# A new instruction order, new buffer slots and other fillers for a fused polysketch-attention and wave-MLP kernel

## The chip, the cores and the metric

The kernel runs on one core of one Trainium2 chip. The metric is the device time of one execution in microseconds; the profile is of one execution of the same program, recorded by the hardware profiler. The core's engines work side by side, each through its own list of instructions in order: PE (TensorE: matmuls, and PEld, the loading of their weights), DVE (VectorE), ACT (ScalarE), POOL (GpSimd) and SP (SyncE, which only issues DMAs here). An engine that needs another's result waits for a semaphore. The results of matmuls go to PSUM, eight banks; everything else lies in SBUF.

## The reference

Four batches, four heads, 1088 positions, head dimension 32 (so a row of 128), sketch size 8. Attention by polynomial sketches comes first, then an MLP that mixes positions.

```python
def phi(x):
    a = np.einsum('rd,bhsd->bhsr', S1, x)
    b = np.einsum('rd,bhsd->bhsr', S2, x)
    return np.einsum('bhsi,bhsj->bhsij', a, b).reshape(*x.shape[:-1], r * r)
q_p, k_p = (phi(q), phi(k))
kv = np.einsum('bhsf,bhsd->bhfd', k_p, v)
z = np.sum(k_p, axis=2)
num = np.einsum('bhsf,bhfd->bhsd', q_p, kv)
den = np.einsum('bhsf,bhf->bhs', q_p, z)[..., None] + 1e-06
x = (num / den), heads joined to rows of 128

theta = x @ w_theta
zr = x * np.cos(theta)
zi = x * np.sin(theta)
y = np.einsum('ts,bsd->btd', w_tok_r, zr) + np.einsum('ts,bsd->btd', w_tok_i, zi)
u = x + y
out = u + np.maximum(u @ w_ch, 0.0)
```

The weights `w_tok_r`, `w_tok_i` (1088 x 1088), `w_theta`, `w_ch`, `S1` and `S2` come as float64. [...]

## The kernel before

The kernel is written as a list of 1022 operations, made by calls of `op(engine, cost, function, writes, reads)`. An operation is one or some instructions on one engine: P is TensorE, V VectorE, A ScalarE, G GpSimd, S SyncE. They are numbered from 0 in the order in which the program text makes them. Nothing is run in that order. `Layout.run` takes three strings from the top of the file: `ORDER` lists all 1022 numbers in the order in which they are issued, so that an engine's own list is what remains of it when the other engines' numbers are struck out; `PLACES` gives each of the 419 temporary buffers its slot within its class (22 slots of class `big`, 5 of `zs`, 6 of `hf`, 8 PSUM banks `ps`, and so on); `SPINS` names operations ahead of which so many filler matmuls are put (`spin`, L379: 384 columns of zeros, bf16, into a PSUM bank that is not read). Semaphores are set where one engine's operation needs another's result, or a slot that another's operation still reads.

The stages, for each batch b:

- Loads (SyncE): k, q and v, 576 KB each (`load`, L614), 17 rows of w_tok, 1088 KB each, and w_sq (both small weight matrices, 256 KB); the last two in `weight` (L583). ScalarE turns each row to float32 in two passes (L584 with the function Prelu, L586 with Copy, about 1.2 us each), and VectorE joins them in two (L588 and L590).
- Scales: operations 4 to 28 bring in S1 and S2 and scale them. Operation 9 is ScalarE's second conversion of them (L424), 10 VectorE's product after it, 16 the scaling itself (L469). Operation 3 is a sine of one number that nobody reads (`warm`, L384).
- Keys (`key_sums`, `kfeatures`), the chains that find the sketches' exact slices (`chain`; 174 is the second product in that of batch 1), and query slices (`query_slices`).
- `levels`: three groups of matmuls per batch (420 to 424 for batch 0, 517 to 521 for batch 1, 648 to 652 for batch 2, 719 to 723 for batch 3), three copies to SBUF by ScalarE (L1002), then ten operations of VectorE that make numerator and denominator, stage "den" (725 to 734 for batch 3).
- `outputs_x`: per group of three chunks of 128 positions an outer product on VectorE, its transpose, the numerator matmul and its copy (L1078; 677 for group 1 of batch 2). Batches 0 and 1 are transposed on TensorE; batches 2 and 3 by DMA (`turned`: VectorE's 32 x 32 transposes at L326, such as 736 for batch 3's group 0; a scatter to DRAM by DMAs that SyncE and ScalarE issue, L333, such as 737 and 738; and one DMA back, L338). Then theta: the matmul with w_theta (685, 696 and 707 for batch 2), for batch 2 the transpose of x by DMA too (686 on VectorE, 687 and 688 the scatter, 689 the way back), the rounding, Abs and two sines on ScalarE (L1114, L1115, L1117; 461 to 463 for group 0 of batch 0, 692 to 694 for group 0 of batch 2) and the product z = x (cos, sin) on VectorE (464, 695).
- Mixing: batches 0 and 1 run 17 rows of w_tok against z (`mix_row`; 482 to 498 are rows 0 to 16 of batch 0, three matmuls of up to 384 columns each). Batches 2 and 3 share seven products by Winograd's scheme (`winograd`, stages m1 to m7; 787 and 815 are the first matmuls of m1 and m2).
- Outputs: `finish` and `finish_turned` add x, multiply by w_ch, apply max and store; 1018 is the last matmul.

Ten fillers stand at the start (operation 1, L382). The order matters in every stage, since each engine waits at the head of its own list.

Of the kernel before, what the change touches and what calls it, by code (L numbers as in the profile page):

```python
# [26 lines left out]
TINY = 2.0**-60  # L27
UP = 256.0
ORDER = (
    "6 4 2 5 44 0 1 45 50 3 47 7 340 8 48 46 11 9 10 49 12 29 58 13 30 70 83 84 64 76 71 14 77 85 96 15 88 72 89 78 "  # L30
    "65 86 90 97 79 16 91 66 159 17 92 26 87 98 67 148 27 93 80 32 18 68 19 73 99 309 25 94 141 20 310 74 95 31 142 "
    "35 149 341 21 101 129 151 160 102 150 40 103 104 161 130 105 342 41 131 106 135 107 43 343 162 197 345 136 108 "
    "360 210 22 137 152 355 305 42 53 344 307 198 315 138 306 313 28 110 109 211 139 132 111 23 314 100 308 212 203 "
    "112 133 316 113 36 69 24 204 114 33 199 213 34 143 115 117 75 116 311 144 59 81 200 118 119 312 317 82 346 120 "
    "191 39 121 37 122 124 123 145 424 60 335 125 38 348 422 375 153 420 423 425 154 214 421 155 347 426 61 427 318 "
    "349 246 156 428 57 126 157 239 319 192 158 356 429 227 127 240 164 128 62 247 165 241 430 167 63 337 166 431 "
    "168 249 134 51 432 242 193 169 228 433 140 336 229 170 434 146 194 233 171 350 230 435 173 56 172 147 436 234 "
    "174 361 443 439 437 175 450 438 176 446 440 444 177 441 447 250 445 453 178 442 248 179 448 180 320 454 357 "
    "457 181 188 451 182 338 459 385 458 452 205 183 251 449 235 184 352 460 252 185 187 186 358 521 461 163 339 "
    "462 517 463 253 359 519 518 217 522 455 520 464 236 465 206 523 456 482 524 467 222 215 525 216 351 468 483 "  # L40
    "526 469 353 365 471 527 223 362 473 354 466 189 470 254 528 255 472 529 484 256 190 530 475 387 224 476 257 "
    "376 531 485 267 532 377 268 533 366 390 540 534 370 536 269 537 543 547 541 535 321 542 363 548 270 550 378 "
    "549 538 544 364 386 218 219 368 539 551 388 545 54 220 477 380 201 221 546 552 367 195 325 554 263 553 379 400 "
    "225 486 556 479 264 326 265 389 322 474 266 487 478 557 371 369 558 323 207 196 324 271 372 373 202 480 208 "
    "395 272 562 374 209 381 563 571 382 570 383 488 327 564 405 384 392 489 275 481 391 231 401 410 393 555 490 "
    "560 403 559 273 394 572 396 491 276 274 328 278 573 402 329 492 398 277 565 574 415 404 397 279 406 493 399 "
    "576 280 561 52 407 281 494 282 408 411 409 566 625 575 626 243 567 579 412 413 495 237 283 414 416 496 285 284 "
    "417 418 497 286 299 287 568 419 288 498 55 289 290 293 291 294 292 577 578 648 569 511 505 512 650 649 226 652 "
    "651 627 653 628 654 629 655 602 295 656 580 657 581 658 603 296 604 659 660 582 258 661 583 499 662 300 232 "
    "500 663 238 330 259 506 630 605 298 664 584 260 585 665 261 586 331 262 671 501 666 667 606 513 332 631 333 "  # L50
    "587 678 334 607 502 588 503 589 301 297 514 608 679 609 672 590 632 842 674 668 591 841 673 592 840 681 633 "
    "719 680 721 720 723 722 244 724 669 245 725 610 675 726 670 504 611 727 612 728 593 729 685 686 594 730 688 "
    "595 731 682 302 732 613 687 676 733 634 734 677 614 697 735 635 699 698 615 736 696 596 689 690 839 616 597 "
    "737 691 683 838 692 303 684 636 304 738 742 637 638 708 701 617 743 709 694 693 639 702 707 695 703 700 618 "
    "710 744 749 815 805 704 750 787 705 788 712 816 745 796 640 711 797 798 751 598 706 817 713 739 641 756 714 "
    "799 715 818 789 752 599 790 515 800 844 516 716 819 619 791 718 801 717 620 820 802 746 806 803 807 753 792 "
    "740 808 741 809 760 821 762 810 763 747 845 754 804 748 843 642 811 764 769 755 643 757 822 771 778 765 621 "
    "772 780 758 812 813 622 759 793 781 766 761 768 823 767 773 644 774 794 835 782 770 645 775 846 795 777 847 "
    "776 784 848 783 855 864 856 836 857 814 858 867 779 849 785 859 875 837 868 860 861 866 893 850 876 894 851 "
    "869 884 870 862 885 871 852 872 853 877 865 886 898 887 854 878 895 879 863 888 874 901 880 896 507 873 889 "  # L60
    "938 911 935 890 881 939 882 786 891 824 912 883 902 892 913 940 825 897 903 826 955 646 914 900 915 830 600 "
    "904 942 601 916 831 956 937 957 899 933 975 647 905 934 946 945 931 943 906 907 508 917 509 947 941 510 918 "
    "936 908 827 948 974 958 976 828 959 832 960 932 834 949 944 833 950 829 961 962 951 963 952 987 953 988 954 "
    "919 909 920 989 623 977 990 624 991 926 964 927 978 910 965 992 979 966 921 968 980 922 981 982 928 983 923 "
    "984 925 924 985 930 993 967 986 994 995 969 996 1007 971 929 1012 1013 1014 997 998 1015 999 1008 1000 1001 "
    "1009 1002 1003 1011 1010 1004 1005 970 1006 1016 1017 972 1018 1019 973 1020 1021 "
)
PLACES = (
    "7 0 1 5 0 10 17 16 14 0 15 5 6 15 18 0 10 3 5 0 11 5 3 4 3 6 3 6 2 2 8 4 4 0 5 12 0 6 12 4 12 4 6 5 4 7 1 5 8 "
    "5 10 8 4 4 1 5 9 0 8 8 5 2 0 4 1 6 10 1 0 1 1 4 2 4 0 3 1 4 6 0 4 3 5 1 3 2 21 2 10 6 5 8 3 5 4 3 5 12 4 1 0 2 "  # L70
    "3 2 9 2 0 6 4 4 1 2 1 0 4 2 3 7 3 5 3 3 5 2 4 4 4 6 4 5 4 1 3 5 0 2 3 5 2 0 8 12 1 7 0 7 0 11 4 2 12 7 2 5 5 8 "
    "3 5 3 1 5 4 2 8 12 3 0 3 2 4 3 5 0 1 0 2 4 4 1 7 4 5 3 0 3 19 0 11 13 2 11 8 2 5 16 0 10 2 1 4 7 4 1 11 0 10 3 "
    "4 1 5 3 15 17 1 20 14 1 17 20 3 0 1 4 15 6 0 18 0 1 10 18 3 10 9 0 10 0 6 1 5 6 0 12 2 0 0 0 6 6 2 2 1 4 4 1 0 "
    "7 0 1 6 5 4 1 4 1 4 5 0 0 3 6 5 0 2 4 4 1 3 7 2 0 3 5 4 21 1 21 4 3 4 2 5 7 2 3 7 4 7 1 2 5 2 2 4 7 2 7 1 3 2 "
    "5 4 1 1 0 2 5 3 4 5 4 0 5 5 0 5 2 3 4 6 12 1 3 1 1 2 4 0 2 3 2 3 3 6 5 0 4 1 2 3 0 0 0 6 3 0 0 3 0 7 10 1 10 3 "
    "1 2 2 0 3 1 1 6 3 0 4 5 0 0 3 5 4 6 4 2 6 5 2 5 3 2 0 5 4 15 7 1 6 5 7 0 5 0 1 5 1 6 7 2 6 0 1 7 3 3 1 4 2 5 2 "
)
SPINS = (
    "70:2 15:3 137:1 211:1 424:2 128:1 168:1 174:2 176:1 521:2 "
)  # L80
WARM = 0
SPLIT = ()
# [1330 lines left out]
```

## Time and profile before

| What | Value |
|---|---|
| Median of 3 runs | 219.76 us (219.3, 219.76, 219.84) |
| Span of the profiled execution | 217.4 us |
| Mean granted TensorE clock | 0.997 |
| DMA traffic | 40.58 MB, mean 187 GB/s |
| Longest waits: ScalarE's L1201 for TensorE | 42.5 us in 3 waits |
| Longest wait of a VectorE instruction in 5 to 100 us | 0.4 us, of L437 for TensorE's L436 |
| TensorE's waits that are put down to one instruction | 4.5 us in the ten largest kinds |

The span runs from the first instruction to the last; the runs' time includes what lies around it. A page gives each engine's busy time; the waits are put down to the semaphore that came last. ScalarE's 42.5 us lie at the end, where it has next to nothing to do. Idle time of an engine that nobody waits for costs nothing.

### The profile page before, as it was taken

The page shows a single profiled execution, that of the slowest core. Times are in us where ns is not written, and L with a number is a line of the kernel's source. Part 1 is how long each engine was busy: PE and PEld are TensorE (multiplying, and loading weights), DVE is VectorE, ACT ScalarE, POOL GpSimd, SP SyncE. Part 2 cuts the span into 40 slices and gives each one's busy share as a digit, 9 for nine tenths or more (in the row PEclk, how much of TensorE's full clock was granted, in tenths as well). Part 3 has the DMA queues.
Part 4 walks back from the last instruction along what each step waited for, and adds up shares of the span by engine and source line. Part 5 has one row for each costly group of instructions (what it writes and reads, how often), then busy time and mean ns, then how long its engine had stood idle before and what let it go on. Part 6 is the DMA issues. An engine that isn't in the chain of part 4 may idle for free.

```text
span 217.4 us, 5063 instructions
## 1 busy us (share of the span) xinstructions
PE 209.3 (96%) x1998; PEld 154.3 (71%) x1998; DVE 181.2 (83%) x408; ACT 111.2 (51%) x214; POOL 22.2 (10%) x44
## 2 busy tenths in 40 slices
PE   7999899999999999999999999999999999999994
PEld 3987786686766686666766575667758788888883
DVE  4899999999999999999599839988138999996542
ACT  3998498899779999983322040354037400000010
POOL 2237000055000000100132000100101000000000
PEclk9999999999999999999999999999999999999998
DMA  5999996869979979894226998599911000045253
GB/s 153 429 406 340 425 399 203 333 224 271 267 276 361 361 264 380 219 198 126 33 36 102 222 137 199 105 156 151 231 78 32 0 0 0 3 66 89 36 79 75
DMA packets 52635, 40.58 MB, mean 187 GB/s; under 512 B 45444, under 2 KB 47108, under 8 KB 50436
## 3 DMA queue, kind: packets, MB, share of 16 engines
q1 hardware_dynamic: 35540, 33.71, 48.7%
q0 software_dynamic: 1728, 4.65, 10.5%
q10 hardware_dynamic: 15344, 1.90, 6.0%
q8 instruction: 15, 0.25, 0.5%
q14 instruction: 8, 0.07, 0.1%
HBM read 30.43 MB, written 5.18 MB: 164 GB/s over the span
## 4 chain that ended last, share of the span: by engine, by line
PE 72%; DVE 12%; ACT 8%; DMA 4%; ACTq 2%; issue 2%; SPq 1%
PE ps L341 66%; DMA big<-q_l 2%; DVE lv L305 2%; PE ps L1064 2%; ACTq L333 2%; PE ps L1098 1%; DMA fx<-g 1%; DVE g L305 1%; DVE big L305 1%; PE ps L967 1%; ACT big L584 1%; ACT big L937 1%; DVE hf L309 1%; DVE zs L305 1%; ACT g L1068 1%
## 5 line engine op out<-in xcount | busy, mean ns | idle before, releaser
L341 PE MATMUL ps<-big,zs 128*128 128x384 f32 (+4 forms) x398 | 109.7, 424 | 0.4 <-DVE zs L305 0.4
L341 PEld LDWEIGHTS ps<-big,zs 128*128 128x128 f32 x398 | 71.4, 190 | 30.3 <-issue 2.6
L1201 ACT COPY g<-ps 128x128 f32<-128x128 f32 (+1 forms) x3 | 0.9, 301 | 42.5 <-PE ps L1193 42.5
L305 DVE CUSTOM_DVE_ANT_0 big<-big,big 128x2176 uint16<-128x2176 uint16 x17 | 21.8, 1287 | 0.4 <-ACT big L586 0.2
L584 ACT ACTIVATE big<-zs 128x1088 f32<-128x1088 f32 x17 | 20.9, 1235 | 2.1 <-DMA zs<-w_tok 1.2
L586 ACT ACTIVATE big<-zs 128x1088 int32<-128x1088 uint32 (+1 forms) x18 | 21.3, 1184 | 0.1
L341 PE MATMUL ps<-big,big 128*64 128x64 f32 (+2 forms) x208 | 20.6, 276 | 0.0
L341 PEld LDWEIGHTS ps<-big,big 128*64 128x64 f32 (+1 forms) x208 | 16.5, 154 | 2.9 <-issue 0.2
L305 DVE TENSOR_TENSOR big<-big,big 128x544 f32<-128x544 f32 x24 | 16.7, 712 | 0.0
L1002 ACT COPY lv<-ps 128x480 f32<-128x480 f32 x12 | 6.3, 563 | 14.2 <-PE ps L341 14.2
L312 DVE SCALAR_TENSOR_TENSOR g<-g,ps 128x384 f32<-128x384 f32 x12 | 6.6, 548 | 8.1 <-ACT g L1111 8.1
L1078 ACT COPY big<-ps 128x384 f32<-128x384 f32 x12 | 5.9, 489 | 14.0 <-PE ps L341 8.3
L309 DVE TENSOR_SCALAR big<-big 128x1088 int32<-128x1088 int32 x17 | 12.2, 724 | 0.6 <-ACT big L584 0.5
L341 PEld LDWEIGHTS ps<-w,big 128*128 128x128 f32 x80 | 10.6, 192 | 2.3 <-ACT g L1068 0.6
L319 POOL DMA_DIRECT2D big<-hf x6 | 5.4, 957 | 63.3 <-DVE g L312 33.8
L319 POOL DMA_DIRECT2D g<-big x6 | 5.2, 920 | 64.8 <-ACT g L1179 34.7
L341 PE MATMUL ps<-w,big 128*128 128x128 f32 x80 | 11.8, 280 | 0.0
L305 DVE TENSOR_TENSOR g<-lv 128x768 f32<-128x768 f32 x12 | 11.2, 945 | 0.0
L341 PE MATMUL ps<-g,sm 128*64 128x384 f32 x48 | 10.1, 507 | 0.2 <-ACT big L1078 0.2
L305 DVE TENSOR_TENSOR zs<-ps,g 128x768 f32<-128x768 f32 (+2 forms) x15 | 9.4, 632 | 1.0 <-PE ps L1098 0.9
L341 PEld LDWEIGHTS <-hf 128*64 128x64 f16 (+1 forms) x288 | 7.7, 110 | 2.9 <-issue 1.7
L379 PE MATMUL ps<-idle 128*128 128x384 bf16 x27 | 7.8, 400 | 1.3 <-POOL idle L381 1.3
(194 smaller groups left out, 336.6 us busy)
## 6 DMA issues: line engine op xcount, KB each, us to landing
zs<-w_tok SPq DMA_DIRECT2D x17, 1088.0 KB, 7.0
big<-k_l SPq DMA_DIRECT2D x6, 576.0 KB, 6.6
big<-hf POOLq DMA_DIRECT2D x6, 576.0 KB, 6.0
big<-v_l SPq DMA_DIRECT2D x4, 576.0 KB, 7.0
g<-fq SPq DMA_DIRECT2D x6, 384.0 KB, 5.2
big<-q_l SPq DMA_DIRECT2D x3, 576.0 KB, 5.1
fq<-g SPq DMA_DIRECT2D x12, 96.0 KB, 4.0
fq<-g ACTq DMA_DIRECT2D x12, 96.0 KB, 4.1
```

Of the source, the lines that this page charges most:

```text
L305: eng.tensor_tensor(out=o, in0=a, in1=b, op=f)
L309: (eng or V).tensor_scalar(out=o, in0=a, scalar1=s1, scalar2=s2, op0=op0, **kw)
L312: (eng or V).scalar_tensor_tensor(out=o, in0=a, scalar=s, in1=b, op0=op0, op1=op1)
L319: op("G", 0.9, lambda: G.dma_start(dst(), src(), accum_op=ALU.add), w, r, fly=fly)
L333: E.dma_start(there().rearrange("(a i) (x b j) -> b i x a j", a=nf, b=nf, j=SQ)[f], blocks()[f * SQ:(f + 1) * SQ].rearrange("i (x a j) -> ...
L341: T.matmul(o, lhs, rhs, start=start, stop=stop, skip_group_check=True)
L379: T.matmul(nowhere() if home is None else view(home, (GW,), F32), idle()[:, 0:P], idle(), start=True, stop=True, skip_group_check=True)
L584: op("A", 0.22 + n * 0.0009, lambda: A.activation(dfn(), words_of(raw(), n)[1].bitcast(F32), AF.Prelu, scale=2.0**-112, alpha=-(2.0**32)), ...
L586: op("A", 0.22 + n * 0.0009, lambda: A.activation(stp(), words_of(raw(), n)[0].bitcast(U32), AF.Copy, scale=2.0**-29), [stp], [raw])
L1002: op("A", act(480), lambda g=g, lp=lp: A.copy(lv().rearrange("p l (c n) -> p l c n", n=HR)[:, :, g * GC:(g + 1) * GC], lp().rearrange("p c ...
L1064: T.transpose(tr()[:, i * P:(i + 1) * P], qp()[:, i * H + 2 * n:i * H + 2 * n + 2].rearrange("p h i j -> p (h i j)"), ident())
L1078: op("A", act(GW), lambda g=g, xp=xp: A.copy(xt()[:, g * GW:(g + 1) * GW], xp()), cells(xt, g * GW, (g + 1) * GW), [xp])
```

## The change

Only the three strings differ. All 1022 operations, their functions and their dependences stay, and so does the rest of the file. `ORDER` is another sequence: of TensorE's 357 operations 34 keep their place in its list, of VectorE's 347 17, of ScalarE's 214 19. `PLACES` gives other slots. `SPINS` has 6 fillers ahead of four operations in place of 16 ahead of ten.

Core of the diff; lines of "..." are left out.

```diff
 ORDER = (
-    "6 4 2 5 44 0 1 45 50 3 47 7 340 8 48 46 11 9 10 49 12 29 58 13 30 70 83 84 64 76 71 14 77 85 96 15 88 72 89 78 "
...
-    "174 361 443 439 437 175 450 438 176 446 440 444 177 441 447 250 445 453 178 442 248 179 448 180 320 454 357 "
...
-    "462 517 463 253 359 519 518 217 522 455 520 464 236 465 206 523 456 482 524 467 222 215 525 216 351 468 483 "
...
-    "719 680 721 720 723 722 244 724 669 245 725 610 675 726 670 504 611 727 612 728 593 729 685 686 594 730 688 "
-    "595 731 682 302 732 613 687 676 733 634 734 677 614 697 735 635 699 698 615 736 696 596 689 690 839 616 597 "
-    "737 691 683 838 692 303 684 636 304 738 742 637 638 708 701 617 743 709 694 693 639 702 707 695 703 700 618 "
-    "710 744 749 815 805 704 750 787 705 788 712 816 745 796 640 711 797 798 751 598 706 817 713 739 641 756 714 "
...
+    "58 4 0 2 5 6 1 44 45 47 48 49 50 7 59 8 340 60 56 11 9 61 12 10 51 13 83 70 29 46 14 76 30 355 71 84 15 77 335 64 "
...
+    "326 128 375 230 315 431 236 211 432 199 171 433 200 242 321 173 172 434 316 174 322 212 435 175 450 176 177 453 178 "
...
+    "463 462 359 519 518 522 353 254 467 255 520 464 402 473 523 468 401 482 354 475 370 524 387 483 476 265 469 525 471 "
...
+    "723 680 681 669 721 670 724 686 614 675 722 688 687 641 725 615 726 642 581 245 727 643 582 728 685 682 729 583 690 "
+    "730 584 731 676 691 732 692 616 689 694 733 585 677 697 586 734 698 699 696 735 683 736 303 587 684 737 738 708 588 "
+    "749 589 709 693 304 590 710 695 591 750 700 787 644 742 752 707 842 592 712 815 713 816 743 788 593 844 711 745 796 "
...
+    "765 761 814 768 621 767 773 830 775 825 835 780 770 774 781 846 3 845 782 855 847 776 783 856 777 848 836 784 779 "
...
 )
 PLACES = (
-    "7 0 1 5 0 10 17 16 14 0 15 5 6 15 18 0 10 3 5 0 11 5 3 4 3 6 3 6 2 2 8 4 4 0 5 12 0 6 12 4 12 4 6 5 4 7 1 5 8 "
...
+    "3 6 2 0 5 11 6 2 12 5 10 18 13 7 20 0 4 7 17 0 3 5 1 5 6 6 2 1 0 5 12 1 7 3 0 7 3 6 4 0 14 6 1 0 12 21 7 10 0 1 3 2 "
...
 )
 SPINS = (
-    "70:2 15:3 137:1 211:1 424:2 128:1 168:1 174:2 176:1 521:2 "
+    "40:1 95:1 137:1 113:3 "
 )
```

## The prediction

> **What bounds the kernel now.** I read the page first, then the busy time by stretches, then the chain of waits, then single stretches of ScalarE and VectorE.
>
> ```profile
> span 217.4 us, 5063 instructions
> PE 209.3 (96%) x1998; PEld 154.3 (71%) x1998; DVE 181.2 (83%) x408; ACT 111.2 (51%) x214; POOL 22.2 (10%) x44
> ...
> L379 PE MATMUL ps<-idle 128*128 128x384 bf16 x27 | 7.8, 400 | 1.3 <-POOL idle L381 1.3
> ```
>
> TensorE is busy for 96% of the span, so it looks like the bound. But a matmul's recorded time is longer than the distance to the next one, and 27 matmuls (L379) are fillers that compute nothing. The stretches say more:
>
> ```profile
> 0.00:40.00 40.00, 36.11 (x705) 29.01 (x706) 35.66 (x124) 31.76 (x73) 8.58 (x29) 1.00 0.86 330
> 40.00:100.00 60.00, 59.34 (x569) 41.10 (x568) 58.65 (x112) 54.05 (x89) 6.81 (x6) 1.00 0.88 281
> 100.00:145.00 45.00, 44.71 (x396) 28.71 (x394) 35.66 (x73) 11.92 (x24) 5.10 (x7) 1.00 0.66 126
> 145.00:200.00 55.00, 54.91 (x250) 43.48 (x251) 43.49 (x84) 12.53 (x26) 1.71 (x2) 1.00 0.35 69
> ```
>
> The columns after the length are PE, PEld, DVE, ACT and POOL busy. From 40 to 100 us VectorE works 58.65 of 60 us and ScalarE 54.05: TensorE is fed by a full VectorE. After 145 us only TensorE is full.
>
> I need TensorE's lost time, which "busy" hides. So I gave each operation the distance from its first matmul's start to the start of the next operation, at the fast end (15th percentile) of all operations of its shape; the fp32 matmuls lie 322 ns apart at 384 columns, 242 at 288, 215 at 256. Over the whole list that makes 198.0 us. An operation's **delay** is its recorded start less the sum ahead of it in the list. Old list: first levels of batch 0 (424) 24.0 - 19.9 = 4.1; second chain product of batch 1 (174) 38.7 - 30.3 = 8.4; last row of batch 0 (498) 100.2 - 87.5 = 12.7; levels of batch 3 (719) 125.2 - 111.7 = 13.5; first Winograd product (815) 145.1 - 130.1 = 15.0; last operation (1018) 213.8 - 197.8 = 16.0. So 12.7 of the 16.0 us are lost in the first 100 us, by VectorE: row 498 started 0.3 us after VectorE had finished row 16 (419, at 99.9). The last named wait is this:
>
> ```profile
> 140.85 1.73 ACTq L333
> 142.57 0.05 issue
> 142.62 0.49 ACT g L1111
> 143.11 0.41 ACT g L1117
> 143.52 0.51 ACT g L1115
> 144.04 0.02 issue
> 144.06 0.97 DVE zs L305
> 145.03 0.04 issue
> 145.07 0.94 PE ps L341 x3
> ```
>
> ScalarE issues DMAs (ACTq) ahead of the sines of batch 2; the product z and the Winograd matmuls wait behind them. From there to the end TensorE waits for nobody.
>
> **The change part by part.** No operation is added or removed except fillers. Every duration below is that of the trace; what changes is what stands ahead of what. For VectorE and ScalarE I summed, in each list, the recorded durations of the operations up to a given one; the trace tells when that sum was reached (VectorE: 41.8 at 40.1 us, 107.8 at 99.8).
>
> *Where the early delay is set.* Ahead of row 498 the old list has 107.9 us of VectorE work and 87.5 of TensorE work; the new one 107.8 and 88.8. VectorE's part is equal, and TensorE has 1.3 us more to do meanwhile: -1.3 if VectorE keeps its pace. Bounds -1.3 and 0. I take -1.3, with the three terms below against it.
>
> *The start.* Operation 58 (w_sq) moves from tenth to first on SP's queue: 0.44 us of issue ahead of st and k0, and 256 KB ahead of them at the 278 GB/s of the first 10 us, 0.9 us. On ScalarE its two conversions (0.46 and 0.42) go ahead of operation 9, and one VectorE step (0.29) ahead of operation 10. Against that the scaling (16) is no longer queued behind the 1.16 us squares of q0. Bounds 0 and 1.4 us; VectorE's sum of 7.0 comes at about 10.7 us by this, where the old trace had 7.5 at 10.5: I take +0.7.
>
> *Neighbours on VectorE.* The two sorts are to be seen here:
>
> ```profile
> 128.70 0.46 DVE L309 TENSOR_SCALAR big<-lv 128x576 f32<-128x576 f32 x1 [4.64 <-ACT lv L1002]
> 129.20 0.76 DVE L305 TENSOR_TENSOR lv<-lv,big 128x576 f32<-128x576 f32 x1
> ...
> 132.62 0.41 DVE L305 TENSOR_TENSOR lv<-big,lv 128x288 f32<-128x288 f32 x1
> 132.96 0.44 DVE L1016 TENSOR_REDUCE sm<-lv 128x36 f32<-128x288 f32 x1
> ```
>
> An instruction that reads what its neighbour wrote starts 0.035 us after it (median of all such pairs); one that doesn't starts 0.084 before its end. Up to the sum of 108 the old list has 10 dependent pairs of neighbours on VectorE, the new one 16: 6 x 0.119 = +0.7 us, bounds 0 and 0.7, since VectorE is full there.
>
> *The activation table.*
>
> ```profile
> 1.58 1.28 ACT L384 ACT_TABLE_LOAD   x1 [1.58 <-DVE hm L366]
> 2.88 0.20 ACT L384 ACTIVATE warm<-halfpi 128x1 f32<-128x1 f32 x1
> 2.99 0.23 ACT L412 ACTIVATE sp<-st 128x48 f32<-128x48 f32 x1
> ```
>
> The only load stands before the sine at L384 (operation 3), and everything after uses that table. The new list moves operation 3 near the end, so a Prelu (L412) comes first and the first real sine is operation 463. Whether the table loaded for Prelu has sines, no row shows: 0 or another 1.28 us at 463. There ScalarE follows VectorE's 460 (sum 55.0, 51.3 us) by some 2.0 us of work, to 53.3; VectorE needs it for 464 (sum 58.6, 54.6 us). 1.3 us of cover hide 1.28; I take +0.1, and 1.28 if the cover is gone.
> The Trainium skill ("ScalarE: Activation LUTs", What ACT_TABLE_LOAD costs) gives 1283 ns for the load, as this row has, and about 1380 ns of draining beside it, 2.66 us for each change of table; no run here shows the drain. By it this term would be 1.4, not 0.1. It speaks against the change.
>
> So row 498 comes at 99.8 + 0.3 + 0.7 + 0.7 + 0.1 = 101.6 less 88.8: delay 12.8, for 12.7.
>
> *ScalarE early.* The new list has more of ScalarE's work early: ahead of product 174 41.6 us of it, not 35.0 (VectorE 41.8, not 40.2). By 38.6 us the old trace had ScalarE busy 30.3, 0.87 of its sum, and idle 8.2, of which 3.7 in the first 10 us and 2.6 waiting for the levels. With no idle time after the start the new list needs 41.6 x 0.87 + 3.7 + 0.7 = 40.6 us, and VectorE comes at 40.1 + 1.4 = 41.5: no cost. With the old 4.5 us of idle time as well, 45.0: VectorE 3.5 later. Bounds 0 and 3.5. The loads are issued earlier in the new list, and the levels start later; nearer to the lower end I take +1.0.
>
> *The Winograd wait.* The transposes of batch 2 (686, then the DMAs 687 and 688) now go ahead of the denominator work of batch 3, 2.7 us earlier. But the second sine (693) now stands on ScalarE behind the DMA issues of 738 (2.19 us), which wait for VectorE's 736. 736 ends 9.5 us after that denominator work starts (old trace: 128.7 to 138.5); 2.2 + 0.6 + 1.0 follow, 13.3 in all. TensorE has 16.3 us from the levels (111.0) to the product (now 787, at 127.3), and the denominator work starts 3.3 us into it: 13.0 left. Wait 0.3, plus VectorE's queue of 0.9: about 1.2 for the 1.5 of before. Bounds -1.5 and +0.6 as change; I take 0.
>
> *Slots and fillers.* New slots bring new waits: theta of group 1 (696) waits for the copy 677, 0.9 us ahead of it. 0, bounds 0 and 0.9. Ten of the 16 single fillers go; at 0.16 us each they stood in TensorE's idle time or where VectorE sets the pace: 0, bounds -1.1 (fillers on the chain of waits) and 0.
> The Trainium skill ("TensorE: Matmul & The Clock Gate", Part 1) says that after an idle window of about 3.4 us TensorE runs at half its clock; five of the fillers that go stood before 7 us. The granted clock was 1.00 in every stretch here; what half a clock would do is the last rival.
>
> *The late part.* From 815 to the end the delay grows by 1.0 with no wait; the new list has VectorE's last sums as close to TensorE's as before. 0, bounds -0.3 and +0.8.
>
> **Sum**: +0.1 (row 498) + 1.0 = +1.1 on 217.4, a span of 218.5. The runs' median, 219.76, is 2.4 above the span: 220.9 us.
>
> **The rivals.** *Faster: VectorE keeps its pace.* If the start, the neighbours and ScalarE cost VectorE nothing, the 1.3 us of TensorE's work count whole, with 0.1 less: 216.0, 218.4 us. For it: VectorE was idle for only 2.0 us between 10 and 100 us in the old list, so there is little for ScalarE to make worse. Against: 16 dependent pairs. It decides if VectorE has done row 16 by 100.5 us.
> *No change: ScalarE is not late.* The 1.0 falls away: 217.5, 219.9 us. For it: 40.6 against 41.5.
> *ScalarE is the bound early.* It idles as before: 3.5 in place of 1.0, 221.0, 223.4 us. For it: its wait of 2.6 us for the levels; against: loads come earlier.
> *The clock drops.* TensorE's work between its sums 4.1 and 9.5 takes twice as long, +5.4; with 0.8 of slack there +4.6: 222.1, 224.5 us. Against: its idle gaps there are near 1 us.
>
> **How the numbers follow.** Forecast 0.36, its own range 220.2 to 222.0; faster 0.34; no change 0.15; ScalarE the bound 0.12; clock 0.03. A difference of 0.3% (0.66 us) is about what a measurement can tell: faster 0.34, same 0.15, slower 0.36 + 0.12 + 0.03 = 0.51. The wait at the Winograd products closing on top of the faster case gives 216.9, so the range starts at 216.6; at the top it takes in ScalarE as the bound, 223.4.
>
> **What would show it.** After: row 498 near 101 to 103 us; product 174 near 42; a second table load just before L1117 near 53 us; 787 near 142; fillers 17 by count. Wrong if VectorE idles little before 100 us and row 498 starts by 100.5, or if 787 starts right behind its neighbour on TensorE with no wait.

## The result, and the profile after

| | Before | After |
|---|---|---|
| Median of the runs | 219.8 us (219.3 to 220.7) | 232.66 us (232.25, 232.58, 232.74, 234.22) |
| Ratio, 95% interval | | 1.061 [1.0563, 1.0657] |
| Span of the profiled execution | 217.4 us | 230.5 us |
| Mean granted TensorE clock | 0.997 | 0.962 |
| First matmul of the scaling (12) starts | 4.51 us | 7.04 us |
| Row 498 starts, and its delay | 100.18 us, 12.6 | 113.55 us, 24.7 |
| First matmul of m1 (787), and its delay | 146.09 us, 15.1 | 154.29 us, 27.0 |
| Last matmul (1018), and its delay | 213.81 us, 16.0 | 226.82 us, 29.0 |

The kernel became 12.9 us slower; the forecast was 1.1. Of the 13.0 us that the last matmul's delay grew, 12.1 are there at row 498. In the new file the lines from `spin` on have numbers smaller by two (L339 is the old L341).

First, the page of the changed kernel: its span, its busy times, the clock in 40 slices of 5.8 us (tenths), and one line of its waits.

```profile
span 230.5 us, 5059 instructions
PE 216.1 (94%) x1988; PEld 159.5 (69%) x1988; DVE 182.4 (79%) x408; ACT 112.4 (49%) x215; POOL 20.0 (9%) x44
PEclk9758998897999999999999999999999999999999
```

```profile
ACT L410 <- DMA st<-s_t: 4.5, 1, 4.5
```

The clock, 1.00 before in all slices but the last, is down to 0.7, 0.5 and 0.8 in slices 2 to 4, to 0.8 in slices 7 and 8 and to 0.7 in slice 10, which ends near 58 us. The last line is a wait: ScalarE's first conversion of S1 and S2 stands for their load. The stretches of the changed kernel that answer to those of before (columns: length, then PE, PEld, DVE, ACT and POOL busy with counts, clock, DMA share, GB/s):

```profile
0.00:40.00 40.00, 32.53 (x508) 25.69 (x510) 29.51 (x112) 29.69 (x64) 12.59 (x35) 0.86 0.96 354
40.00:100.00 60.00, 57.59 (x716) 42.09 (x713) 52.92 (x107) 47.05 (x84) 0.86 (x1) 0.95 0.66 247
100.00:145.00 45.00, 45.00 (x391) 30.03 (x390) 37.44 (x70) 18.84 (x32) 4.76 (x6) 1.00 0.61 118
145.00:200.00 55.00, 53.77 (x242) 38.88 (x241) 43.31 (x81) 16.04 (x35) 1.75 (x2) 1.00 0.48 92
```

In the first 40 us TensorE ran 508 matmuls where it had run 705, and VectorE, busy for 35.66 us before, was idle for 10.5 us. The DMA engines were busier: share 0.96 against 0.86. After 100 us nothing much changed.

Where TensorE's time went in the first 62 us can be summed from one stretch of each kernel, 0 to 62 us:

```profile
0.00:62.00 62.00, 57.93 (x966) 44.25 (x966) 57.45 (x175) 51.09 (x107) 14.53 (x34) 1.00 0.88 311
```

That was before; this is after:

```profile
0.00:62.00 62.00, 52.83 (x834) 41.49 (x835) 46.01 (x155) 42.95 (x94) 12.59 (x35) 0.86 0.90 338
```

Idle: 62 - 57.93 = 4.1 before, 62 - 52.83 = 9.2 after, 5.1 more. Clock: (1 - 0.86) x 62 = 8.7 us of a full clock not granted. Together 13.8, about the whole loss. Three places make up most of it. The first is the start, on ScalarE of the changed kernel (start, us, what, and in brackets the idle time and what ended it):

```profile
4.50 1.28 ACT L410 ACT_TABLE_LOAD   x1 [4.50 <-DMA st<-s_t]
5.79 0.24 ACT L410 ACTIVATE sp<-st 128x48 f32<-128x48 f32 x1
```

Before, the table was loaded from 1.58 to 2.86 us, under the arrival of S1 and S2, and the conversion started at 2.99. Now the load of w_sq goes first, S1 and S2 come 1.5 us later or more, and the table is loaded behind them: 2.8 us in all. TensorE stands from 4.72 to 7.04. The clock follows. These two stretches of the changed kernel, each 3.41 us long, are the one with that gap and the next:

```profile
4.90:8.31 3.41, 0.92 (x7) 0.71 (x7) 1.95 (x12) 3.23 (x9) 0.51 (x2) 1.00 1.01 399
8.31:11.72 3.41, 3.36 (x34) 2.57 (x36) 2.71 (x12) 2.96 (x9) 1.12 (x4) 0.50 1.03 424
```

TensorE was busy for 0.92 of 3.41 us, and then ran at half clock for three such lengths, to 18.5 us. The second place is a stop of TensorE:

```profile
35.40 0.53 PE L339 MATMUL ps<-g,big 128*32 128x64 f32 x21
38.31 0.30 PE L339 MATMUL ps<-g,big 128*32 128x64 f32 x3 [2.38 <-issue]
38.54 0.57 PE L339 MATMUL ps<-mv,hf 128*64 128x96 f16 x18
```

The 24 matmuls are one operation (81). After 21 of them TensorE stands for 2.4 us, and the profile names nothing that it waits for ("issue"). 3.4 us of half clock follow from 39.0. The third place is 52.7 to 56.1 us, half clock again.

### The profile page after: what moved, and what is told of

Same layout as the page of the kernel before. It is cut to its first block, busy times and chain, and to the rows that moved or that the text cites. A ratio compares the mean times of both kernels' runs of the same rounds, so it can differ in the third digit from the quotient of the medians.

```text
span 230.5 us, 5059 instructions
## 1 busy us (share of the span) xinstructions
PE 216.1 (94%) x1988; PEld 159.5 (69%) x1988; DVE 182.4 (79%) x408; ACT 112.4 (49%) x215; POOL 20.0 (9%) x44
## 5 line engine op out<-in xcount | busy, mean ns | idle before, releaser
L339 PE MATMUL ps<-big,zs 128*128 128x384 f32 (+4 forms) x398 | 108.7, 424 | 1.2 <-DVE zs L303 1.2
L339 PEld LDWEIGHTS ps<-big,zs 128*128 128x128 f32 x398 | 71.4, 190 | 30.7 <-DVE zs L303 2.2
L339 PE MATMUL ps<-big,big 128*64 128x64 f32 (+2 forms) x208 | 21.4, 287 | 0.0
L339 PEld LDWEIGHTS ps<-big,big 128*64 128x64 f32 (+1 forms) x208 | 17.0, 164 | 3.0 <-DVE g L310 0.4
L1076 ACT COPY big<-ps 128x384 f32<-128x384 f32 x12 | 5.5, 483 | 17.4 <-PE ps L339 15.1
L339 PEld LDWEIGHTS ps<-w,big 128*128 128x128 f32 x80 | 10.5, 192 | 2.4 <-ACT big L1076 0.7
L1000 ACT COPY lv<-ps 128x480 f32<-128x480 f32 x12 | 6.4, 559 | 11.6 <-PE ps L339 11.6
L339 PE MATMUL ps<-w,big 128*128 128x128 f32 x80 | 11.4, 279 | 0.1
L339 PE MATMUL ps<-g,sm 128*64 128x384 f32 x48 | 9.6, 501 | 0.0
L339 PEld LDWEIGHTS <-hf 128*64 128x64 f16 (+1 forms) x288 | 8.2, 121 | 1.9 <-issue 1.7
L339 PE MATMUL ps<-mf,big 128*64 128x96 f32 x144 | 9.2, 269 | 0.0
```

What stands on the lines that cost most here:

```text
L339: T.matmul(o, lhs, rhs, start=start, stop=stop, skip_group_check=True)
L1000: op("A", act(480), lambda g=g, lp=lp: A.copy(lv().rearrange("p l (c n) -> p l c n", n=HR)[:, :, g * GC:(g + 1) * GC], lp().rearrange("p c ...
L1076: op("A", act(GW), lambda g=g, xp=xp: A.copy(xt()[:, g * GW:(g + 1) * GW], xp()), cells(xt, g * GW, (g + 1) * GW), [xp])
```

## The experiments

All are variants of the changed kernel (a_) or of the kernel before (b_). An edit is a place in `ORDER` or an entry of `SPINS`; the diffs show the neighbourhood of the moved numbers. The time of before ran beside each: 219.4 to 219.8 us. A time is the median of four runs (ten for b_nofill); idle time and clock are those of the one profiled execution.

| Run | Time, us | Ratio, 95% | TensorE idle in 0-62 us | Clock in 0-62 us |
|---|---|---|---|---|
| after | 232.66 | 1.0563 to 1.0657 | 9.2 | 0.86 |
| a_both | 232.0 | 1.0513 to 1.0585 | 10.4 | 0.83 |
| a_sine | 230.52 | 1.0467 to 1.0535 | 11.4 | 0.89 |
| a_fill | 233.16 | 1.0549 to 1.0657 | 11.6 | 0.94 |
| a_v1 | 231.78 | 1.0442 to 1.0612 | 11.4 | 0.89 |
| a_fill_v1 | 233.02 | 1.0514 to 1.0672 | 9.9 | 0.92 |
| a_start_v1 | 232.79 | 1.0488 to 1.0671 | 11.8 | 0.92 |
| a_rows | 238.52 | 1.079 to 1.0915 | 14.9 | 0.84 |
| a_r | 230.56 | 1.04 to 1.0537 | 8.5 | 0.86 |
| a_rows_r | 234.49 | 1.0626 to 1.0733 | 11.7 | 0.86 |
| a_thin | 231.17 | 1.0484 to 1.0564 | 9.9 | 0.89 |
| a_fill_thin | 232.91 | 1.0569 to 1.0656 | 10.9 | 0.89 |
| a_start_r | 229.38 | 1.0391 to 1.0473 | 9.1 | 0.94 |
| a_start_rj | 228.22 | 1.0276 to 1.0415 | 8.0 | 0.94 |
| b_nofill | 219.77 | 0.9968 to 1.0026 | 4.4 | 1.00 |
| b_three | 224.23 | 1.0145 to 1.0262 | 7.2 | 1.00 |
| b_v1late | 223.91 | 1.0091 to 1.025 | 5.6 | 0.94 |
| b_dope2 | 224.96 | 1.0163 to 1.0275 | 6.6 | 0.92 |

### The start

**a_both**: S1 and S2 first, the table early.

```diff
-    "58 4 0 2 5 6 1 44 45 47 48 49 50 7 59 8 340 60 56 11 9 61 12 10 ...
+    "4 0 2 5 6 58 1 3 44 45 47 48 49 50 7 8 340 56 11 9 59 60 12 10 61 ...
```

> The changed kernel with two places put back: w_sq's load (58) goes second on SyncE, behind the load of S1 and S2 (6), with its two conversions (59, 60) behind 9 and its join (61) behind 10; and the sine nobody reads (3) stands at the head of ScalarE's list again. Theory A (the start: S1 and S2 arrive 1.5 us later behind w_sq, the activation table is loaded after them and not under them, TensorE stands idle from 4.72 to 7.04 us, and the clock then falls to half until 18.3 us): the first scaling matmul (12) starts near 4.5 us in place of 7.04, the granted clock of 10 to 20 us is 1.00 in place of 0.57, and the time falls by 2.5 us of start and some 4.1 us of clock, to about 226.1 us. Theory B (the new order has other waits behind the start, which take up whatever the start gives): start and clock as in A, but row 498 still starts within 2 us of 113.6 us and the time is 231 to 233 us. Theory C (the clock has nothing to do with the idle stretch): start near 4.5, clock still near 0.57 in 10 to 20 us, time about 230.2 us.

232.0 us. The start was mended (12 at 4.36 us), but the gap from 4.63 to 5.94 us, before k arrived, was enough for 6.8 us of half clock. And what was gained was lost later: from 41.55 us TensorE stood for v of batch 1. This is TensorE in a_both:

```profile
41.13 0.42 PE L340 MATMUL ps<-sbt,sm 64*64 64x64 f32 x8 [1.85 <-ACT lv L1001]
43.94 0.87 PE L340 MATMUL ps<-g,big 128*32 128x64 f32 x24 [2.39 <-DMA big<-v_l]
```

Theory B: another wait takes it up.

**a_sine**: operation 3 alone put back, behind 1 (`... 5 6 1 3 44 ...`).

> The changed kernel with one place put back: the sine nobody reads (3) at the head of ScalarE's list. Theory A: the table load of 1.28 us lies under the arrival of S1 and S2, which stays at 4.5 us; 12 starts near 5.8 us in place of 7.04, TensorE's idle stretch is 1.1 us in place of 2.3. If the clock falls only after idle stretches of 2 us and more, it stays at 1.00 and the time falls by 1.3 + 4.1 us to about 227.3; if it falls here too, by 1.3 us to about 231.4. Theory B (later waits take it up): 232 to 233 us.

230.52 us, 2.1 less. 12 started at 5.90, the clock stayed at 1.00 to 28.9 us, and then fell for 6.8 us twice. But in this trace 174 came at 52.99 us and 482 at 69.01, later than in the changed kernel (50.83 and 68.29): what the start had gained was gone by then, and where the 2.1 us of the median come from isn't shown. The late start itself scatters: in the other traces that keep it, 12 starts at 6.05 us (a_v1, where the clock held behind it) to 6.96.

**a_fill**: the late start kept, TensorE held busy.

```diff
-    "40:1 95:1 137:1 113:3 "
+    "12:10 15:2 40:1 95:1 137:1 113:3 "
```

> The changed kernel with 12 more fillers, ten ahead of 12 and two ahead of 15, and nothing else: the start stays late (12 near 7.1 us), but TensorE works through 4.72 to 7.04 us. Theory A (the idle stretch halves the clock): the granted clock of 10 to 20 us is 1.00 in place of 0.57 and the time falls by some 4.1 us to about 228.6 us. Theory B: the clock holds, the later waits take it up, 231 to 233 us. Theory C (the clock falls for another reason): 0.57 still, 232.7 us. Beside it: the changed kernel's TensorE stops for 2.4 us at 35.93 us inside operation 81, behind the 962nd of its recorded instructions and between two matmuls of one operation, where nothing is waited for, while a block of 16 KB on the queue of its instructions comes in (35.99 to 36.95 us). If that is a list that ran out of instructions, the stop sits at the same count of instructions from the start, so with 24 instructions more ahead of it it lies 24 earlier in the work (in operation 81's first half or 75), if there is one; if it belongs to operation 81, it stays between the same two matmuls.

233.16 us, as in theory B (0.2 above its range). The clock was 1.00 up to 43.0 us, so the gap does halve it, and operation 420 started 2.7 us sooner (35.81 for 38.54). By operation 128 the gain was gone: 50.70 for 48.57. TensorE's stop moved as theory A's second part had it. This is a_fill's TensorE:

```profile
33.94 0.35 PE L340 MATMUL ps<-g,big 128*32 128x64 f32 x9
35.45 0.43 PE L340 MATMUL ps<-g,big 128*32 128x64 f32 x15 [1.16 <-issue]
```

Operation 81 again, but after 9 of its matmuls and not 21: 12 matmuls and 12 weight loads earlier, just as many as the fillers put ahead. The stop is at the 962nd recorded instruction of TensorE's list, not at a place of the work.

**b_three** and **b_nofill**: the same doubts, put into the kernel before.

```diff
-    "6 4 2 5 44 0 1 45 50 3 47 7 340 ... 29 58 13 ... 775 846 795 ...   70:2 15:3 137:1 211:1 ...
+    "58 6 4 2 5 44 0 1 45 50 47 7 340 ... 29 13 ... 775 846 3 795 ...   137:1 211:1 ...
```

(b_nofill has the last part only.)

> The kernel before with the three things of the changed kernel's start: w_sq's load (58) first on SyncE, the sine nobody reads (3) late (behind 846), and no fillers ahead of 70 and 15. Theory A: 12 starts near 7.0 us, TensorE is idle for some 2.3 us before it, the clock falls to about half for some 10 us, and the time rises by 2.5 + 4.1 us to about 226.4 us. Theory B (the start matters only in the changed kernel's order; here later slack takes it up): 219.8 to 222 us. Theory C (late start but no fall of the clock): about 222.3 us.

> The kernel before without the five fillers ahead of 70 and 15, nothing else. Theory A (without them TensorE's idle share in 4.7 to 8 us halves the clock): the clock falls to half somewhere in 8 to 15 us and the time rises by 1.7 to 5 us, to 221.5 to 225 us. Theory of the prediction (fillers cost and bring nothing): 219.2 to 220.3 us.

b_nofill 219.77 us: the five fillers bring and cost nothing there, and the clock stayed at 1.00. b_three 224.23 us, 4.4 more. This is b_three's TensorE:

```profile
3.56 1.17 PE L378 MATMUL ps<-idle 128*128 128x384 bf16 x3
7.53 0.37 PE L435 MATMUL ps<-ident,m 128*2 128x128 f32 x1 [2.81 <-DVE m L454]
```

12 starts at 7.53 after 2.8 us of idle time, and yet the clock did not fall: theory C, at a larger price than its 2.5. The late start alone, without clock and without the new sequence, is worth 4.4 us in the kernel before.

### One late load

**a_v1**, **a_fill_v1**, **a_start_v1**: v of batch 1 right behind v of batch 0.

```diff
-    "... 83 70 29 46 14 76 30 355 71 84 15 77 335 64 85 16 57 88 78 345 96 17 86 360 62 53 18 ...
+    "... 83 70 29 46 53 14 76 30 355 71 84 15 77 335 64 85 16 57 88 78 345 96 17 86 360 62 18 ...
```

> The changed kernel with one load moved on SyncE's list: v of batch 1 (53) right behind v of batch 0 (46), so ahead of w_tok's rows 4, 0, 2 and 5 and of batch 3's load 57; it landed at 43.8 us in the changed kernel and in every variant of it so far, against 29.05 us before, and TensorE's sum of it (134) starts at 43.5 to 43.9 us in all of them. Theory D (the late landing is what the other variants ran into; in the changed kernel itself TensorE comes to 134 only 0.3 us ahead of the landing): the load lands near 25 us, and the time hardly moves, 231.5 to 232.7 us. Theory E (the landing has nothing to do with it): the same time, and moving it will not help where the start is mended either. Theory F (the landing is the whole loss): 222 to 226 us.

> The changed kernel with the 12 fillers of a_fill and v of batch 1 loaded behind v of batch 0. In a_fill TensorE was 6.4 us further on by row work up to operation 113, reached 134 at 40.8 us, stood for 2.7 us until the load landed at 43.5, and ran at half clock from 43 to 49 us. Theory D: 134 starts near 40.8 us, no stop and no half clock behind it, operation 128 near 45.5 us in place of 50.7, and the time is 233.2 - 5 = about 228 us (226.5 to 229.5). Theory E (another wait takes its place at once): 231 to 233 us.

> The changed kernel with all three: S1 and S2 loaded first and the table loaded under their arrival (as in a_both), fillers ahead of 70 (four) and 15 (three), and v of batch 1 behind v of batch 0. Theory D: 12 starts near 4.4 us, the clock stays at 1.00 up to 40 us, 134 comes some 2 us sooner than in a_fill_v1, and the time is about 226 us (224 to 228): what is left over the kernel before, 6 us, is the sequence itself between 12 and 420. Theory E: 231 to 233 us. If the sequence itself costs nothing, 220 to 222 us.

231.78, 233.02 and 232.79 us. The first fits theories D and E alike; the other two are theory E. The load landed at 23 to 25 us, and the wait went elsewhere. In a_start_v1, w_tok's row 4, now behind it in the queue, held ScalarE:

```profile
22.87 0.33 ACT L797 ACTIVATE sm<-sm,kg 128x64 f32<-128x64 f32 x1
28.86 1.18 ACT L583 ACTIVATE big<-zs 128x1088 f32<-128x1088 f32 x1 [5.66 <-DMA zs<-w_tok]
```

Chain 0's operation 110 stands behind this row's conversions on ScalarE's list, and TensorE stood for 4.5 us ahead of 111. Then came the stops at the block ends, the 962nd and, as here, the 1218th instruction (962 + 256):

```profile
43.09 0.52 PE L340 MATMUL ps<-g,big 128*32 128x64 f32 x19
46.02 0.31 PE L340 MATMUL ps<-g,big 128*32 128x64 f32 x5 [2.40 <-issue]
```

**b_v1late**: the same load made late in the kernel before (`... 428 57 53 126 ...`, from between 42 and 344).

> The kernel before with one load moved: v of batch 1 (53) from the 14th place of SyncE's list to behind 57, some 13 us later. Its first use (134) stood at 35.5 us. Theory D: the load lands near 38 to 41 us in place of 29.05, 134 and what follows stand for 2.5 to 5 us, the clock falls behind the stop for 3.3 us or more (another 1.6), and the time rises by 3 to 6 us, to 223 to 226 us. Theory E (slack takes it up): 219.5 to 221 us.

223.91 us, 4.4 more, theory D. This is its TensorE:

```profile
35.06 0.67 PE L340 MATMUL ps<-sbt,sm 64*64 64x64 f32 x8 [0.38 <-ACT sm L797]
37.67 0.87 PE L340 MATMUL ps<-g,big 128*32 128x64 f32 x24 [1.94 <-DMA big<-v_l]
```

134 stands 1.94 us for the load, and 6.8 us of half clock run from 36.2.

### The traffic

**a_r**: the second loads of k late, and three joins with them.

```diff
-    "... 50 7 59 8 340 60 56 11 ... 85 16 57 88 ... 103 104 311 350 356 105 344 ...
+    "... 50 7 59 8 340 60 11 ... 85 16 88 ... 103 104 311 350 56 57 216 356 105 344 ...
```

> The changed kernel with the second loads of k of batches 2 and 3 (56, 57) moved from the 8th and 15th place of SyncE's list to behind row 3's load (350), and with them the three joins behind 216 on GpSimd's list, so that some 1.7 MB of software DMA leaves the stretch of 23 to 40 us. Theory H: v of batch 1 lands before 41 us in place of 43.8, the instruction block behind the 962nd comes before 33 us in place of 36.9, and the time falls by 1 to 4 us, to 229 to 231.5 us. Theory E: 232 to 233 us.

230.56 us, 2.1 less. v of batch 1 landed at 34.2 us; the block still came only at 35.0 to 36.1, against the expectation, and TensorE stood 2.1 us for it.

**a_rows** and **a_rows_r**: conversions of rows 4, 0, 2 later.

```diff
+    "... 168 423 356 357 358 400 134 ... 63 194 336 337 338 385 229 ... 434 316 346 347 348 349 365 174 ...
```

> The changed kernel with the conversions of w_tok's rows 4, 0 and 2 on ScalarE and VectorE (356 to 358, 336 to 338, 346 to 349) moved back behind 423, 194 and 316, some 15 to 20 us later, and the loads that take their slots (rows 13, 10, 6: 400, 385, 365) with them. Theory H (the changed sequence asks for more bytes before 57 us than the DMA engines move; what stands waiting for late loads at the head of ScalarE's list holds chain 0, and TensorE's own instruction blocks of 256, which come through the same engines, arrive 6 to 12 us after they are asked for): ScalarE no longer stands for row 4 ahead of chain 0, the block behind the 962nd recorded instruction comes before 33 us, and the time falls to 227 to 231 us; the late start and the half clock of 8 to 18 us remain. Theory E (another wait takes each one's place): 231 to 233 us.

> All of it together: start and fillers as in a_start_v1, v of batch 1 behind v of batch 0, the second loads of k late as in a_r, rows 4, 0 and 2 late as in a_rows. Theory H: no block of instructions comes more than 5 us after it is asked for, TensorE has no stop at the 706th, 962nd or 1218th recorded instruction, the clock stays at 1.00 up to 60 us, and the time is 221 to 225 us. Theory E, or the sequence's own dependences: 229 to 233 us.

238.52 and 234.49 us: worse, against both theories. The rows' conversions now stood in the way between 44 and 60 us, where TensorE was idle for 3.6 us in one piece (54.0 to 57.6 in a_rows) and at half clock. The edit does not separate the theories.

**b_dope** (260.2 us) has no verdict: the added code stood outside the block that keeps the written order, so the whole program was ordered anew, and its copies went out at 4.5 to 16 us. **b_dope2** is the same with the order kept.

```diff
+        def more():
+            last()
+            for j in range(4):
+                G.dma_start(extra[j], v[j].rearrange("p c h d -> p (c h d)"))
+        L.ops[34].fn = more
```

> The kernel before with four copies of 576 KB from v to places in DRAM that nobody reads, issued by GpSimd behind operation 34 at about 20 us; nothing waits for them, and it computes what it computed. In the kernel before no block of TensorE's instructions came later than 3.9 us after it was asked for in 20 to 60 us (the one behind the 1218th, 28.2 to 32.0 us), and none held TensorE. Theory H: with the DMA engines fuller from 20 to 35 us the blocks come 6 us and more after they are asked for, TensorE stops at the 962nd or the 1218th recorded instruction and nowhere else for it, the clock halves behind it, loads land some 5 us later, and the time rises by 2 to 6 us, to 222 to 226 us. Theory E (bytes that nobody waits for cost nothing): 219.3 to 220.5 us.

> The kernel before, its own sequence unchanged this time (in b_dope the instructions stood outside the written order and were ordered anew, so it says nothing), with four copies of 576 KB from v to places in DRAM that nobody reads, issued by GpSimd behind operation 34 at about 20 us. Nothing waits for them. Theory H: the DMA engines, full in 20 to 33 us and two thirds full to 45 us, stay full for some 6 to 10 us more; TensorE's instruction blocks come 6 us and more after they are asked for in place of 1.1 to 3.9; TensorE stops at the 962nd or the 1218th recorded instruction, the clock halves behind the stop, v of batch 1 lands some 3 us later, and the time rises by 1.5 to 6 us, to 221 to 226 us. Theory E (bytes that nobody waits for cost nothing): 219.3 to 220.5 us.

224.96 us, 5.2 more, from 2.3 MB that nobody waits for (issued at 20.24 us). So bytes alone cost time here. But the way was not the one named: the instruction blocks came as before (3.6 us after 28.3), and TensorE had no stop at the 962nd or 1218th instruction. ScalarE stood for rows of w_tok in b_dope2 (engine, tile and line; releaser; us in total, times, longest):

```profile
ACT big L585 <- DMA zs<-w_tok: 2.8, 1, 2.8
ACT big L583 <- DMA zs<-w_tok: 0.9, 1, 0.9
```

TensorE stood behind a copy of ScalarE's for 2.35 us, and half clock followed for 10.2 us:

```profile
39.00:49.00 10.00, 9.31 (x68) 7.22 (x69) 5.47 (x16) 6.11 (x15) 0.00 (x0) 0.50 0.74 284
```

**a_thin** and **a_fill_thin**: bytes taken away.

```diff
-        op("S", n * 0.00255, lambda: SY.dma_start(raw(), src), [raw], [])
+        c = n // 8 if len(L.ops) in (400, 385, 365, 375) else n
+        op("S", n * 0.00255, lambda: SY.dma_start(raw()[:, :c], src[:, :c]), [raw], [])
```

> The changed kernel in which the loads of w_tok's rows 13, 10, 6 and 8 (400, 385, 365, 375; issued at 28 to 48 us, used from 85 us on) bring only the first eighth of each row, and the conversions read that eighth eight times over, so that these four rows of the mixing are not the reference's; every instruction stays, in its order and with its size, and 3.8 MB of traffic leaves the stretch of 28 to 58 us. Theory H: v of batch 1 lands before 41 us, the blocks behind the 962nd and the 1218th recorded instruction come sooner, and the time falls by 1 to 4 us, to 228.5 to 231.5 us, with the late start and the half clock of 8 to 18 us still in it. Theory E (the sequence's own dependences are the bound): 232 to 233.5 us.

> a_fill and a_thin together: TensorE kept at full clock by fillers through the start, and the four rows' loads an eighth of their size. a_fill by itself was 233.2 us, since what it gained by 40 us it lost standing for v of batch 1 and for its instructions. Theory H: the gain of a_fill now stays, 134 starts before 41 us, and the time is 226 to 230 us. Theory E: 232 to 233.5 us.

231.17 and 232.91 us. a_thin is inside theory H's range by its time, but not by its reason: v of batch 1 came no sooner (134 at 44.5 us), and the block behind the 962nd instruction came at 35.5 to 36.4, as in the changed kernel. What it saved was the third fall of the clock, at 52.7 us. a_fill_thin is theory E. The four loads were issued at 28 us and later, behind v of batch 1 on SyncE's queue, and hadn't delayed it. That holds for this one queue: GpSimd's copies in b_dope2 were issued behind that load too (20.24 us against 17.94), and it took 17.2 us to land where it had taken 10.3:

```profile
big<-v_l SPq DMA_DIRECT2D x1, 576.0 KB, 17.2
```

**a_start_r** and **a_start_rj**: start and load order together, then the last early join moved too.

```diff
-    "... 33 31 217 163 ... 131 252 ... 253 ...   40:1 95:1 137:1 113:3
+    "... 33 31 163 ... 350 56 57 216 217 356 ... 131 252 253 ...   70:4 15:3 40:1 95:1 137:1 113:3
```

(a_start_r leaves 217 and 253 in their places; both have a_both's start.)

> The changed kernel with the start of a_start_v1 (S1 and S2 first, table early, fillers ahead of 70 and 15) and the second loads of k late as in a_r; v of batch 1 stays in its place. a_r by itself gained 2.1 us, a_start_v1 nothing: there row 4 of w_tok landed at 28.8 us, behind v of batch 1, and ScalarE stood at its conversion with chain 0 behind it. Theory H: row 4 lands near 22.5 us and v of batch 1 near 34 us, operation 111 starts before 28 us in place of 31.8, and the time is 225.5 to 229 us. Theory E: 230 to 233 us.

> a_start_r with the last join of the early stretch (217, issued at 17.6 us and landing 11 us later) moved on GpSimd's list behind 216, and 253 behind 252, so that no software DMA runs before the second load of k arrives at 39 us. In a_start_r TensorE still stood 2.2 us at its 962nd and 2.4 us at its 1218th recorded instruction, at half clock for 6.8 us behind them: 8 us of what it lacks of the kernel before. In all variants so far the block behind the 962nd came 5.7 to 11.5 us after it was asked for with one to two joins under way, the blocks around it 2.5 to 4.3 us. Theory H1 (the software DMA lengthens this block's wait): the block comes before 31 us in place of 33.0 to 34.1, the stop at the 962nd instruction is under 0.5 us, and the time falls by 1.5 to 5 us, to 224.5 to 228 us. Theory H2 (the block's wait comes from SyncE's loads alone): the stop stays at 2 us and the time at 229 to 230.5 us. Theory E: the stop goes and 229 to 231 us remain, since TensorE then stands the longer at the 1218th.

229.38 us: 3.3 less than the changed kernel, 0.4 above theory H's range; 111 started at 27.99, as it expected. a_start_rj: 228.22 us. Its profiled execution took 227.63 us and four runs spread from 226.37 to 230.38, so its gain over a_start_r is not certain. The block behind the 962nd instruction came at 31.2 us, 4.5 after it was asked for in place of 6.5, and the stop there was gone, which speaks for H1, though block and time are each 0.2 above its bounds. The one at the 1218th stayed, as theory E had it; this is a_start_rj:

```profile
37.02 0.52 PE L340 MATMUL ps<-g,big 128*32 128x64 f32 x19
39.82 0.33 PE L340 MATMUL ps<-g,big 128*32 128x64 f32 x5 [2.27 <-issue]
```

No version beat the kernel before. The best got back 4.4 of the 12.9 us.

## Why the prediction was wrong, step by step

**The direction was right; two steps failed. The first is *the start*, with the clock behind it:** 12 came 2.5 us late where the term had 0.7, and the half clock that followed had a chance of 0.03. In the changed kernel's own trace most of the loss is there before 40 us. Reckoned like the prediction's delays, 424 (24.02 us before, 39.86 after) is some 11 us further behind; this is an estimate from the two traces. It holds the start, its half clock, and TensorE's stop that ends at 38.31, which no term had.

**The second is *ScalarE early*, where loads were taken as help; it is why mending the start gained little.** It said: "The loads are issued earlier in the new list, and the levels start later; nearer to the lower end I take +1.0." But the DMA engines were already busy for 0.86 of the first 40 us (0.96 after), and what is issued early stands ahead of the rest. Between v of batch 0 and v of batch 1 SyncE now issues four rows and a second load of k, and two more 576 KB loads (56, 51) stand ahead of both. The landing stands in the trace of before; this is its DMA view of the one load issued at 18.7 us, and the last column is us to landing:

```profile
big<-v_l SPq DMA_DIRECT2D x1, 576.0 KB, 10.3
```

And this is the same load in a_both, issued at 18.8 us:

```profile
big<-v_l SPq DMA_DIRECT2D x1, 576.0 KB, 25.0
```

Landed at 29.05 before, at 43.8 in a_both, and its first reader on TensorE (134) starts at 43.68 us in the changed kernel where it started at 35.54. The bound of the term was 3.5 us. In the changed kernel itself TensorE had lost that time already and stood only 0.29 us ahead of 134:

```profile
43.68 0.54 PE L339 MATMUL ps<-g,big 128*32 128x64 f32 x24 [0.29 <-DVE sm L303]
```

So the two bounds end together, and product 174 came at 50.83 us, not near 42: delay 18.5, 10.1 more than before. That this is a limit in time and not in work is argued from what mending did: in the changed kernel and in a_both, a_sine, a_fill, a_v1, a_fill_v1 and a_start_v1 operation 113 starts anywhere from 29.3 to 34.0 us, but 128 at 48.6 to 51.7 and 482 at 68.3 to 70.2. Three waits follow one another there (the load of v, rows at the head of ScalarE's list, TensorE's own instructions), and taking away one left the others. b_v1late and b_dope2 show the same from the other side: one late load, or 2.3 MB more, each cost the kernel before 4.4 to 5.2 us. What holds the 8.4 us that the best variant still lacks stays open.

**The start, +0.7.** The first part was well sized: 0.44 + 0.9 us later for S1 and S2, measured 1.5 or more (4.50 for 2.99 or sooner; 3.51 to 4.42 in the other traces with this start). The mis-sized term is *the activation table*: 0.1, since I looked at its second load, near 53 us. It stood at 64.47 us, ScalarE's work on both sides of it without a gap:

```profile
64.10 0.36 ACT L796 ACTIVATE sm<-sm,kg 128x64 f32<-128x64 f32 x1
64.47 1.28 ACT L1115 ACT_TABLE_LOAD   x1
65.76 0.52 ACT L1115 ACTIVATE g<-g 128x384 f32<-128x384 f32 x1
```

But the first load was the dear one: with the sine gone from the head of the list it stands behind the wait for S1 and S2, 1.28 us in series. In the kernel before, b_three prices the late start (12 at 7.53) at 4.4 us.

The Trainium skill ("ScalarE: Activation LUTs", What ACT_TABLE_LOAD costs) adds about 1380 ns of draining to each load. This trace doesn't agree: its neighbours above stand 0.01 us from it on either side.

**The clock, a rival at 0.03 (+4.6).** It was priced on the old list's gaps ("near 1 us"), though the start term itself makes a longer one. It happened, three times over, 17 us at half clock in 0 to 62 us. A rival that sits on top of another term should have had that term's chance.

**Order, -1.3.** TensorE does have 88.8 us of work ahead of row 498, as counted. But VectorE didn't keep its pace: idle for 100 - 29.51 - 52.92 = 17.6 us of the first 100, before 5.7. Row 498 came at 113.55, not 101.6.

**Dependent neighbours on VectorE, +0.7**: not tried by itself; with VectorE idle that long it can't be read.

**Fillers, 0**: right for the five at the start, by b_nofill (0.9968 to 1.0026); the other five that go were not tried. **Slots, 0**: not tried by themselves either, since every a_ variant keeps the new slots and every b_ variant the old ones. 17 fillers are left, as counted:

```profile
L377 PE MATMUL ps<-idle 128*128 128x384 bf16 x17 | 5.5, 453 | 1.3 <-POOL idle L379 1.3
```

**Winograd wait, 0, and late part, 0 (-0.3 to +0.8).** From 719 to 787 the delay grew by 1.61 us, before by 1.60: as forecast, though the working had 9.5 us where its own two times (128.7 to 138.5) make 9.8. But a wait that neither term had stands further on, at 808 in m2. The chain that ended last in the changed kernel shows it (start, us, what):

```profile
163.96 0.52 ACT g L1113
164.48 0.02 issue
164.50 0.97 DVE zs L303
165.47 0.04 issue
165.52 15.72 PE ps L339 x78
```

TensorE stood 0.8 us for the last sine of batch 2 and the product after it, where the old chain had this wait at 815. From 719 to 1018 the delay grew by 3.6 us, before by 2.5.

## What to carry to other kernels

When an order changes, list the loads in their queue with their bytes, and ask when each lands and what stands behind its first reader; a load that goes earlier makes the ones behind it later. A wait at the very start can cost more than its length: 3.0 us cost 4.4 in b_three, and in the changed kernel 2.3 us of idle TensorE were followed by 10.2 us of half clock. If mending one wait moves the end by nothing, look whether all variants reach one operation at the same time: then something with a fixed supply may be the bound, and single repairs won't show what they are worth.

## What the runs showed of the hardware

**TensorE can run out of instructions.** Its list comes through a DMA queue of its own (queue and kind, packets, MB, share of the 16 engines; the changed kernel):

```profile
q8 instruction: 15, 0.25, 0.4%
```

Fifteen packets of 16 KB. Stops named "issue", of 0.7 to 2.4 us, stood at the 706th, 962nd or 1218th recorded instruction, 256 apart, in 12 of 14 traces of the changed kernel and its variants, at whatever matmul was there (21, 14 or 9 of 24, according to the fillers ahead), and in none of the kernel before. Four more of that name, of 2.3 to 4.5 us, stood ahead of operation 111 and are no such ends; in a_start_v1 that was the wait for ScalarE. I take a block to be asked for when TensorE begins the one ahead of it; that is inferred. By it a block came 0.3 to 0.7 us after the request with less busy DMA engines (asked for at 35.6 and 43.6 us in before), 3.3 to 3.8 us with full ones (22.6 and 28.2 us), and 4.5 to 11.5 behind the 962nd instruction in the changed kernel and its variants; where TensorE stood for it, its first instruction ran 1.2 to 1.6 us after it was in. The Trainium skill ("Runtime: NRT & Kernel Launch", Instruction fetch mechanics) has the 16 KiB blocks of 256 instructions and calls the cost of crossing one mostly hidden. The counts agree; the cost here was up to 2.4 us for a crossing, and half clock behind it. Why one block waits 11 us and its neighbour 4 stays open; a_start_rj, one trace, speaks for software DMA under way as one cause.

**The clock falls in steps of 3.41 us.** In 16 traces every stretch of half clock but the last, at the end of the run, was 1 to 4 times 3.41 us long, and those of one trace began whole multiples of 3.41 us apart. In 22 of 34 cases TensorE had been busy for less than half of the length ahead (0.92 of 3.41 us above), in 11 for 0.50 to 0.73 of it, and in one for 0.84 (a_fill_thin, at 11.06 us); behind 0.47 it held once (a_rows, from 35.5 us). So no threshold follows. In b_three the clock held although idle time filled about half of one length, and the rest of it fell into the next (lengths counted back from its only fall, at 224.96 us):

```profile
3.05:6.46 3.41, 1.67 (x6) 0.47 (x4) 0.00 (x0) 1.46 (x2) 0.00 (x0) 1.00 0.91 305
6.46:9.87 3.41, 2.34 (x11) 2.04 (x11) 2.65 (x16) 1.52 (x6) 0.98 (x2) 1.00 1.05 435
```

The Trainium skill ("TensorE: Matmul & The Clock Gate", Part 1) has a free-running window of 3413 ns and says that one idle window halves the clock; the length agrees, but the window need not be idle: a gap of 1.3 us was enough in a_both.
